# Moving the third unit's inverse, its key normalization and the first layer input's transposes in a fused delta-rule attention and MLP kernel

## The chip, the core and the metric

The kernel runs on one core of one Trainium2 chip. A core has five engines that run their own instruction lists in order: TensorE (PE in the rows, its weight loads PEld), VectorE (DVE), ScalarE (ACT), GpSimd (POOL) and SyncE (SP), which here only issues transfers. An engine waits when its next instruction needs something that another engine or a transfer has not delivered yet, and everything behind that instruction waits with it. The metric is the device time of one execution in microseconds; less is better.

## What is computed

Two stages, the second fed by the first. For each of 4 x 8 heads a 48 x 48 state is carried over 768 steps by a delta rule, and the outputs go through a two-layer MLP with a squared ReLU.

```python
B, H, S, D = 4, 8, 768, 48          # batch, heads, steps, head size
k_n = k / (norm(k, axis=-1) + 1e-06)
for t in range(S):
    y[:, :, t] = einsum('bhd,bhde->bhe', q[:, :, t], state)
    v_old = einsum('bhde,bhd->bhe', state, k_n[:, :, t])
    state += beta[:, :, t] * einsum('bhd,bhe->bhde', k_n[:, :, t], v[:, :, t] - v_old)
x = y as (3072, 384)                # 3072 tokens, d_model 384, d_ff 2048
h = maximum(x @ w_in, 0.0)
out = (h * h) @ w_out
```

## The kernel before

The 768 steps are cut into 12 units of 64 steps. For one unit the 64 sequential updates become dense products, a triangular inverse and a short chain on the carried state:

- `load` and `load_q` fetch the keys into `kpad` (three buffers in turn) and the queries into `qpad` (one buffer). `normalize` squares the keys (L290, ACT), sums (L294, DVE), takes roots and reciprocals, and scales `kpad` (L306, DVE).
- `static` turns keys and queries on TensorE (L342), copies them to `kq` (L345, ACT), forms key-key and query-key products (L358), masks them into `ap` (L368, DVE) and sends the part to be inverted through DRAM (`blocks`, L376) back into `lt` in another layout (L386). Its last step also issues the loads of the values `vt` (L247), of the next unit's queries (L253) and of the step sizes `bt` (L274, L276).
- `invert` is forward substitution on DVE: 31 steps of one multiply (L514) and one subtract (L515), then a scaling (L517). The result `z` is written to DRAM as `inv` (L521) and loaded back twice: into `tt` (L525) and `t1t` (L530). The first two units share `invert_both`, whose last part, on 16 x 16 quarters with TensorE (L468, L475), ends with the transfers `t1t` and `tt` at L488 and L493.
- `state_part` is the chain of a unit: L567 multiplies `ap` with `tt`; L604 reads the state with keys and then queries; L612 subtracts from `vt`; L578, L628, L645 and L656 follow, L650 adds to `state`, L660 copies the outputs `y`.
- `moe` is the MLP of a unit: transposes of `y` (L676), split into a high and a low part (L679, L680), first layer (L710), squared ReLU (L717, L718), split (L720, L689), second layer (L697), results (L732) to the output (L738). The matrices are split too: `split_weights` handles 28 weight pieces (`w0` to `w27`) through L141 to L173 before and during the second unit.

The order on every engine is written out by hand: the scheduler follows the order in which the program issues. Ahead of the loop this is a list of `take(part, n)`, which runs n steps of a generator. In the loop `weave` sorts the steps of all parts by a place between 0 and 1 of the unit's period, the time between two units. `steps(n, a, b)` spreads n steps evenly from a to b. The 32 steps of an inverse begin at `I0` (`J0` for the third unit, whose inverse runs in the second unit's period) and end at `I1` (`J1`), where a value above 1 means that the rest, the list `left`, falls into the unit's own period. Units are counted from one in this text, so the third unit is `u == 2` in the code.

Of the kernel before, what the change touches and what calls it, by code (L numbers as in the profile page):

```python
# [8 lines left out]
F32 = mybir.dt.float32  # L9
# [12 lines left out]
def kernel(  # L22
# [22 lines left out]
    nc = tc.nc  # L45
    B, H, S, D = q.shape
    DM, DF = w_in.shape
    P = 128
    C = 64
    HB = 32  # L50
    QB = HB // 2
    NC = 2
    NP = H // 2
# [8 lines left out]
    apool = ctx.enter_context(tc.tile_pool(name="attn", bufs=2))  # L62
# [39 lines left out]
    state = const.tile([P, 2, NC, NP, D], F32, name="state")  # L102
# [179 lines left out]
    def normalize(d):  # L282

        n2, s0, s1 = [apool.tile([P, H2], F32, name=f"{n}{d['u'] % 2}", bufs=1) for n in ("n2", "s0", "s1")]
        kn = d["kp"].rearrange("p c h d -> p (c h) d")[:, :, :D]
        squares = []
        for c in range(NC):
            sq = (apool.tile([P, H, D], F32, name="y", bufs=2) if d["u"] in (2, 3) else
                  spool.tile([P, PC], F32, name="rest", bufs=3)[:, :H * D].rearrange("p (h e) -> p h e", h=H))
            nc.scalar.activation(out=sq, in_=kn[:, c * H:(c + 1) * H], func=AF.Square)  # L290
            squares.append(sq)
# [24 lines left out]
    def static(d):  # L316

        u = d["u"]
# [3 lines left out]

        kq = apool.tile([P, NC, NP, 2, 2, C], F32, name="kq", bufs=2)
        ap = apool.tile([P, NC, H, 2, C], F32, name="ap", bufs=2)
# [102 lines left out]
    def invert_both():  # L427
# [26 lines left out]
        dd = apool.tile([P, HB, HB], F32, name="lt", bufs=1)  # L454
        nc.vector.transpose(out=dd.rearrange("p r t -> p t r"), in_=z.rearrange("p j t -> p t j"))
        parts = [dd[:, x * H2:(x + 1) * H2] for x in range(2)]
# [175 lines left out]
    def onward(d):  # L632
# [30 lines left out]
        if not u:  # L663
            for b in range(2):
                nc.scalar.copy(out=state[:, b], in_=ku[b])

# [73 lines left out]
    def take(gen, n=None):  # L740
        while n is None or n > 0:
            try:
                next(gen)
            except StopIteration:
                return
            if n is not None:
                n -= 1

    def steps(n, a, b):

        return [a + (b - a) * (m + 0.5) / n for m in range(n)]
# [32 lines left out]
    I0, I1, NI = 0.47, 1.14, HB  # L784
    J0, J1 = 0.56, 1.22
    units = S // C
    ds_ = []
# [4 lines left out]
    with tc.manual_schedule(engines=engines):  # L792
# [58 lines left out]
        take(splits, 3)  # L851
        take(chain, 1)
        take(pair[1], 1)
        load_q(ds_[2])
        take(splits, 3)
        first, third = moe(ds_[0]), normalize(ds_[2])
        take(first, 1)
        take(inverse, 1)
        take(splits, 3)
        split_early = False  # L860
        used = 6 + 2 + 3 + 4 + 3 * 3
        before = None
        corner, inverse = inverse, None
        for u in range(1, units):
            parts = []
            ends = (J0, J1) if u == 1 else (I0, I1)
            n_i = round((1 - ends[0]) / (ends[1] - ends[0]) * NI)
            if inverse:
# [3 lines left out]
            if u < units - 1:  # L872
                parts.append((static(ds_[u + 1]), [-1, 0.155, 0.165] if u > 1 else [0.16, 0.255, 0.265]))
            inverse = invert(ds_[u + 1]) if u < units - 1 else None
            if inverse:
                parts.append((inverse, steps(n_i, ends[0], 1)))
                left = steps(NI - n_i, 0, ends[1] - 1) + [ends[1] - 0.98]
            if u == 1:
                parts.append((corner, [0.03, 0.06, 0.07]))
                parts.append((third, [0.02, 0.04, 0.05, 0.075, 0.085, 0.1]))  # L880
                parts.append((late_loads(), [0.08]))
                parts.append((splits, steps(3 * (NW - FIRST) + 3 - used, 0, 0.72)))
                parts.append((pair[1], [0.25]))
# [41 lines left out]
```

## Time and profile before

| what | value |
|---|---|
| the times of three runs | 647.45, 650.03 and 936.88 us |
| their median | 650.03 us |
| the profiled execution | 647.84 us |
| its span, first to last instruction | 646.0 us |
| what lies outside the span | 1.84 us |
| mean granted TensorE clock | 0.952 |
| TensorE busy | 588.8 us (91%) |
| VectorE busy | 416.7 us (64%) |
| ScalarE busy | 317.3 us (49%) |

Times in the rows are microseconds from the span's start. [...] The span falls into a start of about 70 us, the second unit's period, in which the rest of the weights is split, up to about 150 us, and the units after that, which repeat every 45 us.

### The profile page before, as it was taken

The numbers are of one execution on the slowest core, as the hardware profiler recorded it, in microseconds if no ns is written. First come the engines' busy times: TensorE is split into PE (matmuls) and PEld (weight loads), VectorE is DVE, ScalarE is ACT, GpSimd is POOL, SyncE is SP. The second block draws the span as 40 slices with busy tenths as digits, with TensorE's granted clock in tenths as the row PEclk, the third lists the DMA queues.
The fourth block names the chain that finished last, engine by engine and source line by source line (L and its number), as shares of the span: only waits on it lengthen the run. The fifth ranks groups of instructions, "written<-read, shape, count | busy, mean of one in ns | idle before, by whom it ended". The sixth has DMA issues, their size and how long they took to land.

```text
span 646.0 us, 23872 instructions
## 1 busy us (share of the span) xinstructions
PE 588.8 (91%) x10392; PEld 557.9 (86%) x10392; DVE 416.7 (64%) x1128; ACT 317.3 (49%) x623; POOL 29.6 (5%) x52
## 2 busy tenths in 40 slices
PE   2848978994399999999999999999999999999997
PEld 2536867994399999999999999999999999999997
DVE  4785779792269488587685795794885875841121
ACT  4746766543053644545454445436445454445442
POOL 4000100000100100001001001001001010000000
PEclk9956698998599999999999999999999999999999
DMA  7787635016301722623524526217226134030100
GB/s 224 202 274 158 200 66 95 7 25 96 67 6 31 121 54 42 110 55 53 91 52 66 92 40 114 55 31 121 55 40 114 30 51 92 3 67 2 25 1 25
DMA packets 172464, 49.32 MB, mean 76 GB/s; under 512 B 164288, under 2 KB 167368, under 8 KB 172360
## 3 DMA queue, kind: packets, MB, share of 16 engines
q1 hardware_dynamic: 168840, 47.06, 36.2%
q8 instruction: 82, 1.34, 0.9%
q10 hardware_dynamic: 3392, 0.72, 0.6%
q14 instruction: 22, 0.18, 0.1%
q0 software_dynamic: 128, 0.01, 0.0%
HBM read 36.54 MB, written 10.49 MB: 73 GB/s over the span
## 4 chain that ended last, share of the span: by engine, by line
PE 81%; DVE 6%; ACT 4%; SPq 3%; DMA 3%; issue 2%; DVEq 0%; ACTq 0%
PE o L697 31%; PE h L710 30%; PE x L604 2%; PE g L604 2%; PE x L628 2%; PE x L358 2%; PE g L656 2%; PE g L358 1%; PE x L645 1%; PE x L578 1%; PE h L567 1%; PE h L676 1%; PE x L342 1%; DMA kpad<-in_k_dram 1%; PE o L166 1%
## 5 line engine op out<-in xcount | busy, mean ns | idle before, releaser
L697 PE MATMUL o<-w,h_h 128*128 128x384 f32 x768 | 204.5, 348 | 0.0
L710 PE MATMUL h<-x_h,w 128*128 128x256 f32 x1152 | 171.7, 285 | 0.0
L717 ACT ACTIVATE r<-h 128x512 f32<-128x512 f32 x96 | 57.5, 599 | 227.5 <-PE h L710 227.4
L689 DVE TENSOR_TENSOR h_l<-r,h_h 128x512 fp32r<-128x512 f32 x96 | 66.5, 692 | 147.8 <-ACT h_h L720 147.6
L710 PEld LDWEIGHTS h<-x_h,w 128*128 128x128 f32 x1152 | 156.7, 191 | 1.4 <-issue 0.2
L697 PEld LDWEIGHTS o<-w,h_h 128*128 128x128 f32 x768 | 135.1, 189 | 3.2
L697 PE MATMUL o<-w,h_l 128*128 128x384 f32 x384 | 130.6, 340 | 0.0
L710 PE MATMUL h<-x_l,w 128*128 128x256 f32 x576 | 100.9, 284 | 0.0
L514 DVE SCALAR_TENSOR_TENSOR tmp<-lt,bt,z 128x126 f32<-128x126 f32 (+22 forms) x310 | 95.8, 309 | 7.7
L515 DVE TENSOR_TENSOR z<-z,tmp 128x126 f32<-128x126 f32 (+22 forms) x310 | 79.2, 255 | 10.6
L710 PEld LDWEIGHTS h<-x_l,w 128*128 128x128 f32 x576 | 83.1, 192 | 0.0
L697 PEld LDWEIGHTS o<-w,h_l 128*128 128x128 f32 x384 | 72.7, 189 | 0.0
L718 ACT ACTIVATE r<-r 128x512 f32<-128x512 f32 x96 | 60.7, 633 | 3.0
L720 ACT CAST h_h<-r 128x512 fp32r<-128x512 f32 x96 | 59.5, 620 | 3.1
L503 POOL MEMSET z<- 128x512 f32 x10 | 5.3, 525 | 467.8 <-DMA inv<-z 434.7
L567 PEld LDWEIGHTS h<-tt,ap 32*32 32x32 f32 x704 | 7.6, 109 | 21.6 <-issue 20.5
L567 PE MATMUL h<-tt,ap 32*32 32x32 f32 x704 | 9.0, 198 | 18.7 <-DMA tt<-inv 18.7
L650 DVE TENSOR_TENSOR state<-state,x 48x384 f32<-48x384 f32 x40 | 22.0, 551 | 0.9 <-PE x L645 0.3
L358 PE MATMUL x<-kq 48*64 48x64 f32 (+1 forms) x608 | 19.1, 250 | 1.4 <-ACT kq L345 0.7
L358 PEld LDWEIGHTS x<-kq 48*64 48x64 f32 x608 | 16.6, 147 | 3.4 <-ACT kq L345 1.1
L342 PE MATMUL x<-plus,kpad 64*128 64x64 f32 x96 | 6.7, 241 | 13.9 <-DVE kpad L306 11.2
L342 PEld LDWEIGHTS x<-plus,kpad 64*128 64x128 f32 x96 | 5.4, 152 | 14.3 <-issue 11.5
(141 smaller groups left out, 651.6 us busy)
## 6 DMA issues: line engine op xcount, KB each, us to landing
w<-in_moe_w_in_dram SPq DMA_DIRECT2D x12, 512.0 KB
w<-in_moe_w_out_dram SPq DMA_DIRECT2D x16, 384.0 KB
lt<-blocks SPq DMA_DIRECT2D x20, 256.0 KB
qpad<-in_q_dram SPq DMA_DIRECT2D x96, 48.0 KB
vt<-in_v_dram SPq DMA_DIRECT2D x48, 96.0 KB
out_dram<-a SPq DMA_DIRECT2D x46, 96.0 KB
kpad<-in_k_dram SPq DMA_DIRECT2D x88, 48.0 KB
blocks<-ap SPq DMA_DIRECT2D x40, 64.0 KB
```

The lines of the kernel that those rows point to most:

```text
L358: nc.tensor.matmul(ps[j][to * C:(to + 1) * C, p, (x - first) * C:(x - first + m) * C], lhsT=kq[rows, c, p, b, 0], rhs=kq[rows, c, p, b, x: ...
L514: nc.vector.scalar_tensor_tensor(out=tmp, scalar=bt[:, s:s + 1], op0=ALU.mult, op1=ALU.mult, **factors)
L515: nc.vector.tensor_tensor(out=z[:, :nj, s + 1:], in0=z[:, :nj, s + 1:], in1=tmp, op=ALU.subtract)
L567: nc.tensor.matmul(ps[at[h % 2][b], h // 2], lhsT=ap[lower[b], c, e, 0, :HB], rhs=tt[lower[b], c, e, HB:], start=True, stop=True)
L604: nc.tensor.matmul(dst[j][to, c, p], lhsT=d["kq"][rows, c, p, b, x], rhs=state[rows, b, c, p], start=(c == 0 and p == 0) if x else True, s ...
L650: nc.vector.tensor_tensor(out=state[rows, b], in0=state[rows, b], in1=ku[b][rows], op=ALU.add)
L689: nc.vector.tensor_tensor(out=h_l, in0=r, in1=h_h.bitcast(F32), op=ALU.subtract)
L697: nc.tensor.matmul(o[i], lhsT=a[:, e, i * P:(i + 1) * P], rhs=halves["wo", ft][w], start=(ft == 0 and n == 0), stop=(ft == FT - 1 and n == 2))
L710: nc.tensor.matmul(hp[:, e], lhsT=halves["wi", (kt, ft // EACH)][w][:, f], rhs=x[:, kt], start=(n == 0), stop=(n == 3 * KT - 1))
L717: nc.scalar.activation(out=r, in_=hp, func=AF.Relu)
L718: nc.scalar.activation(out=r, in_=r, func=AF.Square)
L720: nc.scalar.copy(out=h_h, in_=r)
```

## The change

Seven things change, five of them only in the order.

- The inverse of the third unit now ends at place 1.14, as those of the other units do (`J1` is gone), and begins at 0.54 where it was 0.56. With 32 steps, 25 of them now fall into the second unit's period (21 before), 7 into the third's, and the loads of `tt` and `t1t` stand at place 0.16, ahead of the step of `static` at 0.165.
- The third unit's keys are normalized earlier: two of the six steps ahead of the loop, four at places 0.01 to 0.045. Its squares are written into `kq` of the same unit, which `static` fills later, where they were written into two `y` buffers.
- The third unit's `static` stands at 0.12, 0.2 and 0.21, where it was at 0.16, 0.255 and 0.265.
- The first layer input's transposes (`take(first, 1)`) stand right behind the copies of the first unit's `y`, ahead of the second unit's query products.
- The first unit's state is copied by DVE (line L665 before, L669 after) and no longer by ACT.
- The last part of the shared inverse stands at 0.04, 0.09 and 0.1 (0.03, 0.06, 0.07), so its loads at L488 and L493 come behind those of `late_loads` (0.08) and of the fourth unit's keys (0.09).
- The transpose at L455 is cut into two halves, the half that the matmuls at L468 read first.

```diff
         squares = []
+        if d["u"] == 2:
+            d["kq"] = apool.tile([P, NC, NP, 2, 2, C], F32, name="kq", bufs=2)
         for c in range(NC):
-            sq = (apool.tile([P, H, D], F32, name="y", bufs=2) if d["u"] in (2, 3) else
+            sq = (d["kq"][:, c].rearrange("p n i b t -> p (n i b t)")[:, :H * D].rearrange("p (h e) -> p h e", h=H)
+                  if d["u"] == 2 else apool.tile([P, H, D], F32, name="y", bufs=2) if d["u"] == 3 else
...
-        kq = apool.tile([P, NC, NP, 2, 2, C], F32, name="kq", bufs=2)
+        kq = d["kq"] if u == 2 else apool.tile([P, NC, NP, 2, 2, C], F32, name="kq", bufs=2)
...
-        nc.vector.transpose(out=dd.rearrange("p r t -> p t r"), in_=z.rearrange("p j t -> p t j"))
+        for t in (slice(QB, HB), slice(0, QB)):
+            nc.vector.transpose(out=dd[:, :, t].rearrange("p r t -> p t r"), in_=z[:, :, t].rearrange("p j t -> p t j"))
...
-                nc.scalar.copy(out=state[:, b], in_=ku[b])
+                nc.vector.tensor_copy(out=state[:, b], in_=ku[b])
...
-    J0, J1 = 0.56, 1.22
+    J0 = 0.54
...
         take(chain, 1)
+        take(splits, 1)
+        first, third = moe(ds_[0]), normalize(ds_[2])
+        take(first, 1)
+        take(splits, 2)
         take(pair[1], 1)
         load_q(ds_[2])
-        take(splits, 3)
-        first, third = moe(ds_[0]), normalize(ds_[2])
-        take(first, 1)
+        take(third, 1)
+        take(splits, 1)
+        take(third, 1)
         take(inverse, 1)
-        take(splits, 3)
+        take(splits, 2)
...
-            ends = (J0, J1) if u == 1 else (I0, I1)
-            n_i = round((1 - ends[0]) / (ends[1] - ends[0]) * NI)
+            begun = J0 if u == 1 else I0
+            n_i = round((1 - begun) / (I1 - begun) * NI)
...
-                parts.append((static(ds_[u + 1]), [-1, 0.155, 0.165] if u > 1 else [0.16, 0.255, 0.265]))
+                parts.append((static(ds_[u + 1]), [-1, 0.155, 0.165] if u > 1 else [0.12, 0.2, 0.21]))
...
-                left = steps(NI - n_i, 0, ends[1] - 1) + [ends[1] - 0.98]
+                left = steps(NI - n_i, 0, I1 - 1) + [0.16]
             if u == 1:
-                parts.append((corner, [0.03, 0.06, 0.07]))
-                parts.append((third, [0.02, 0.04, 0.05, 0.075, 0.085, 0.1]))
+                parts.append((corner, [0.04, 0.09, 0.1]))
+                parts.append((third, [0.01, 0.015, 0.03, 0.045]))
```

On SP, in the third unit's period, the transfers of its inverse (`inv`, `tt_108`, `t1t`) and those of the fourth unit (`blocks`, `lt`, `vt`) stand like this before. `out_dram<-a` is the first unit's result.

```order
L253 DMA kpad_102<-in_k_dram 64x4x48 x8
L376 DMA blocks<-ap 32x16x32 x4
L386 DMA lt<-blocks 64x1024 x2
L247 DMA vt<-in_v_dram 64x8x48 x4
L253 DMA qpad<-in_q_dram 64x4x48 x8
L274 DMA bt<-in_beta_dram 16x1x32 x4
L276 DMA bt<-bt 64x32
L521 DMA inv<-z 1024x1x32 x2
L738 DMA out_dram<-a 64x384 x4
L525 DMA tt_108<-inv 32x16x32 x4
L530 DMA t1t<-inv 32x8x32 x4
```

The same stretch of SP now, with the line numbers of the changed kernel, where they are 3 or 4 higher:

```order
L253 DMA kpad_102<-in_k_dram 64x4x48 x8
L525 DMA inv<-z 1024x1x32 x2
L379 DMA blocks<-ap 32x16x32 x4
L529 DMA tt_108<-inv 32x16x32 x4
L534 DMA t1t<-inv 32x8x32 x4
L389 DMA lt<-blocks 64x1024 x2
L247 DMA vt<-in_v_dram 64x8x48 x4
L253 DMA qpad<-in_q_dram 64x4x48 x8
```

The loads of `tt` stood behind 29 other issues from `blocks` on and now stand behind six, the two stores of `inv` among them.

On DVE, at the end of the third unit's inverse (L514, L515, L517), with the fourth unit's masking (L368), before:

```order
L515 TENSOR_TENSOR z<-z,tmp 128x15x3
L368 TENSOR_TENSOR ap<-x,mask 128x4x128 x2
L368 TENSOR_TENSOR ap<-g,mask 128x4x128 x2
L514 SCALAR_TENSOR_TENSOR tmp<-lt,bt,z 128x30
L515 TENSOR_TENSOR z<-z,tmp 128x15x2
L689 TENSOR_TENSOR h_l<-r,h_h 128x512
L514 SCALAR_TENSOR_TENSOR tmp<-lt,bt,z 128x16
L515 TENSOR_TENSOR z<-z,tmp 128x16
L732 COPY a<-o_1179 128x384
L517 TENSOR_TENSOR z<-z,bt 128x512
```

The same place of DVE now (L518, L519 and L521 are the inverse, L371 the masking):

```order
L519 TENSOR_TENSOR z<-z,tmp 128x15x3
L518 SCALAR_TENSOR_TENSOR tmp<-lt,bt,z 128x30
L519 TENSOR_TENSOR z<-z,tmp 128x15x2
L518 SCALAR_TENSOR_TENSOR tmp<-lt,bt,z 128x16
L519 TENSOR_TENSOR z<-z,tmp 128x16
L521 TENSOR_TENSOR z<-z,bt 128x512
L371 TENSOR_TENSOR ap<-x,mask 128x4x128 x2
L371 TENSOR_TENSOR ap<-g,mask 128x4x128 x2
L693 TENSOR_TENSOR h_l<-r,h_h 128x512
```

The four masking instructions, one subtraction of the MLP and the copy of a result have moved from ahead of the inverse's last instruction to behind it.

On ACT, early in the second unit's period, the copies of the third unit's turned keys and queries (L345) stand behind three eviction steps of weight pieces and two ReLU groups before (the row ahead of these is the first ReLU group's `L720`):

```order
L141 ACTIVATE w_778<-w_778 128x384
L159 CAST w_1318<-a 128x384
L168 CAST w_1166<-x 128x512
L717 ACTIVATE r<-h 128x512
L718 ACTIVATE r<-r 128x512
L720 CAST h_h<-r 128x512
L141 ACTIVATE w_780<-w_780 128x384
L159 CAST w_1370<-a 128x384
L168 CAST w_1198<-x 128x512
L345 COPY kq<-x 128x2x4x64 x2
L345 COPY kq<-g 128x2x4x64 x2
```

And now:

```order
L141 ACTIVATE w_779<-w_779 128x384
L159 CAST w_1312<-a 128x384
L168 CAST w_1175<-x 128x512
L348 COPY kq<-x 128x2x4x64 x2
L348 COPY kq<-g 128x2x4x64 x2
L721 ACTIVATE r<-h 128x512
L722 ACTIVATE r<-r 128x512
L724 CAST h_h<-r 128x512
L141 ACTIVATE w_781<-w_781 128x384
L159 CAST w_1411<-a 128x384
L168 CAST w_1203<-x 128x512
```

The copies to `kq` have moved ahead of the second ReLU group and of the eviction of weight piece 16 (`w_1198` before, `w_1203` now); on TensorE the transposes at L342 have moved in the same way, to right behind piece 15.

## Rows read from the trace of the kernel before

**Rows 1.** TensorE in order of time around its longest wait (start, us, instruction, [idle before])

```profile
152.33 0.34 PE L697 MATMUL o<-w,h_l 128*128 128x384 f32 x1
170.61 0.28 PE L567 MATMUL h<-tt,ap 32*32 32x32 f32 x2 [17.95 <-DMA tt<-inv]
171.63 1.07 PE L567 MATMUL h<-tt,ap 32*32 32x32 f32 x62 [0.74 <-DMA tt<-inv]
```

**Rows 2.** SP in order of time, 30 to 175 us (issue time, not the transfer's)

```profile
144.33 3.05 SPq L376 DMA_DIRECT2D blocks<-ap  x4
149.11 1.12 SPq L386 DMA_DIRECT2D lt<-blocks  x2
163.23 1.28 SPq L521 DMA_DIRECT2D inv<-z  x2
167.49 2.17 SPq L525 DMA_DIRECT2D tt<-inv  x4
```

**Rows 3.** The chain that ended last, 100 to 186 us (start, us, what)

```profile
169.18 2.41 DMA tt<-inv
```

**Rows 4.** Stretch 170 to 180 us: busy of each engine, granted clock, DMA share, GB/s

```profile
170.00:180.00 10.00, 8.65 (x155) 8.39 (x156) 3.26 (x11) 0.75 (x3) 0.00 (x0) 0.58 0.16 25
```

**Rows 5.** The chain that ended last, whole span: the state products of later units

```profile
220.37 1.09 PE x L604 x64
...
265.95 1.08 PE x L604 x64
```

**Rows 6.** TensorE in the fourth unit's period

```profile
219.62 0.75 PE L567 MATMUL h<-tt,ap 32*32 32x32 f32 x64
```

**Rows 7.** SP in the fourth unit's period

```profile
207.85 2.15 SPq L521 DMA_DIRECT2D inv<-z  x2
...
212.56 2.05 SPq L525 DMA_DIRECT2D tt<-inv  x4
```

**Rows 8.** DVE at the third unit's inverse, its first instruction and its end

```profile
110.32 0.24 DVE L514 SCALAR_TENSOR_TENSOR tmp<-lt,bt,z 128x31 f32<-128x31 f32 x1
...
141.83 1.28 DVE L368 TENSOR_TENSOR ap<-x,mask 128x512 f32<-128x512 f32 x2
143.02 1.28 DVE L368 TENSOR_TENSOR ap<-g,mask 128x512 f32<-128x512 f32 x2
...
145.05 0.69 DVE L689 TENSOR_TENSOR h_l<-r,h_h 128x512 fp32r<-128x512 f32 x1 [0.36 <-ACT h_h L720]
...
146.03 0.55 DVE L732 COPY a<-o 128x384 f32<-128x384 f32 x1
146.50 0.68 DVE L517 TENSOR_TENSOR z<-z,bt 128x512 f32<-128x512 f32 x1
```

**Rows 9.** TensorE in order of time, 36 to 101 us

```profile
41.30 1.90 PE L468 MATMUL h<-lt,ap 32*32 32x16 f32 x128 [1.73 <-DVE lt L455]
...
48.35 1.04 PE L475 MATMUL x<-t,h_h 16*32 16x16 f32 x60 [3.52 <-issue]
...
84.17 0.46 PE L342 MATMUL x<-plus,kpad 64*128 64x64 f32 x7 [2.67 <-ACT w L168]
...
100.80 0.75 PE L567 MATMUL h<-tt,ap 32*32 32x32 f32 x64
```

**Rows 10.** ACT in order of time, 36 to 155 us

```profile
63.57 0.86 ACT L660 COPY y<-g 128x384 f32<-128x384 f32 x2 [0.90 <-PE g L656]
...
79.80 0.59 ACT L168 CAST w<-x 128x512 fp32r<-128x512 f32 x1
...
84.86 1.08 ACT L345 COPY kq<-x 128x512 f32<-128x512 f32 x2 [0.75 <-PE x L342]
```

**Rows 11.** SP early in the second unit's period

```profile
75.72 2.60 SPq L488 DMA_DIRECT2D t1t<-lt  x4
...
89.21 5.89 SPq L253 DMA_DIRECT2D kpad<-in_k_dram  x8
```

**Rows 12.** Instructions on the third unit's key tile, issue ns min/median/max

```profile
L253 SPq DMA_DIRECT2D kpad<-in_k_dram x8: 599/620/1620, 56.0 to 62.1; - x8
```

More of the change, by code (lines that the diff above doesn't have):

```diff
@@ L852 @@
         take(chain, 1)
+        take(splits, 1)
+        first, third = moe(ds_[0]), normalize(ds_[2])
+        take(first, 1)
+        take(splits, 2)
         take(pair[1], 1)
         load_q(ds_[2])
-        take(splits, 3)
-        first, third = moe(ds_[0]), normalize(ds_[2])
-        take(first, 1)
+        take(third, 1)
+        take(splits, 1)
+        take(third, 1)
         take(inverse, 1)
-        take(splits, 3)
+        take(splits, 2)
         split_early = False
-        used = 6 + 2 + 3 + 4 + 3 * 3
+        used = 6 + 2 + 3 + 4 + 3 + 3 + 3
         before = None
@@ L872 @@
             if u < units - 1:
-                parts.append((static(ds_[u + 1]), [-1, 0.155, 0.165] if u > 1 else [0.16, 0.255, 0.265]))
+                parts.append((static(ds_[u + 1]), [-1, 0.155, 0.165] if u > 1 else [0.12, 0.2, 0.21]))
             inverse = invert(ds_[u + 1]) if u < units - 1 else None
             if inverse:
-                parts.append((inverse, steps(n_i, ends[0], 1)))
-                left = steps(NI - n_i, 0, ends[1] - 1) + [ends[1] - 0.98]
+                parts.append((inverse, steps(n_i, begun, 1)))
+                left = steps(NI - n_i, 0, I1 - 1) + [0.16]
             if u == 1:
-                parts.append((corner, [0.03, 0.06, 0.07]))
-                parts.append((third, [0.02, 0.04, 0.05, 0.075, 0.085, 0.1]))
+                parts.append((corner, [0.04, 0.09, 0.1]))
+                parts.append((third, [0.01, 0.015, 0.03, 0.045]))
                 parts.append((late_loads(), [0.08]))
```

## Prediction, on record before the changed kernel's times and trace were seen

> **What bounds the kernel now.** I read the page first: TensorE is busy 91% of the span, and in the slices behind 180 us it is never idle, so a gain has to come from the start or from the third unit. The list of TensorE's waits then has one entry that stands out, and the order of time shows it: the last matmul ends at 152.67, the next, L567 of the third unit, begins at 170.61, after 17.95 us of waiting for `tt<-inv`, and 0.74 more follow between its first two matmuls and the rest [rows 1]. [...]
>
> Why `tt` is late is read on SP. `z`, the inverse, is done on DVE at 147.18 [rows 8], but its store is issued at 163.23 only, and the load of `tt` at 167.49 [rows 2]. In between SP works off the fourth unit's transfers, beginning with `lt<-blocks` at 149.11. So the wait is a queue's, not DVE's. The last load lands 2.41 after its issue at 169.18 [rows 3], at 171.59, and TensorE goes on at once. In the fourth unit SP has another order: `inv` is issued at 207.85, as soon as `z` is there, the `tt` loads end at 212.56 + 2.05 = 214.61 [rows 7], and L567 runs at 219.62 without a wait [rows 6].
>
> Ahead of that gap TensorE works without a break from about 115 us on, so a gain made earlier passes through to 152.67 only if it is made on TensorE itself. The one long wait there is 2.67 us at L342, ended by the eviction L168 of a weight piece on ACT [rows 9].
>
> **The part that carries the forecast: the third unit's inverse.** SP now issues `inv`, four `blocks`, then `tt`. The inverse has the same 32 steps, so DVE's work up to L517 shrinks by what now stands behind it: the maskings from 141.83 to 144.30 (2.47), the subtraction L689 with the 0.36 of idle time before it (1.05), and the copy L732 up to the start of L517 (0.47) [rows 8], together 4.0 us. L517 then begins at 142.5 and ends at 143.2. From `inv`'s issue to the last `tt` issue the fourth unit needs 214.61 - 207.85 = 6.76 [rows 7]; with the landing of 2.41 [rows 3] `tt` is there at 152.4. TensorE arrives at 152.67, or 0.8 earlier by the next part, at 151.9. I take a new wait of 0.5 us. Its bounds are 0, if the steps that now begin earlier fill idle time of DVE, and 4.5, if L517 stays at 147.18: then `tt` lands at 156.35.
>
> What the old wait is worth is read from periods, because the low clock is in it: L604 begins at 220.37 in the fourth unit and at 265.95 in the fifth [rows 5], 45.58 apart. From L567 to L604 take 0.75 [rows 6]. Without the gap the third unit's L604 begins at 152.67 + 0.75 = 153.42 and the fourth's at 199.00, that is **21.4 us** earlier than 220.37. [...]
>
> [...]
>
> **The keys and `static` of the third unit.** The squares go from `y` to `kq` with the same two ACT instructions and the same two sums: 0. The buffer is free, since its last reader, the first unit's products, ran ahead of 40 us. The key load was issued by 62.7, and ACT gets to the squares at about 69. With the keys normalized earlier, the transposes L342 move ahead of one group of nine matmuls and of weight piece 16. Today they wait for that piece's eviction until 84.17 [rows 9]; piece 15 is evicted from 79.80 to 80.39 [rows 10], and L342 would follow it at about 80.8 after arriving at 80.0: 1.9 of the 2.67 are gone. But ACT now takes the four `kq` copies, two of them 1.08 [rows 10], ahead of the second ReLU group and of piece 16's eviction, and the products L358 need the bank that this eviction frees: TensorE ends L342 at 82.0, nine matmuls and the piece's products at 83.9, eighteen more at 86.1; ACT ends the copies at 84.0, the ReLU group of three at 85.9 and, after two instructions of the split, the eviction at 87.4. That is a wait of 1.3 where there are 0.6 now. Net gain 1.2.
>
> **The transposes of `y`.** They now stand right behind ACT's copies, which run from 63.57 to 64.43 [rows 10]. TensorE would reach them at 63.5 and wait 0.9; the second unit's query products, which covered that time, come later and must wait until both `h` banks are read. This costs about 0.4 on TensorE. In exchange DVE and ACT get the first layer's input 2 us earlier, which nothing on TensorE takes up, since the matmuls in front of L710 are the same. The state copy on DVE costs DVE some 1.1 where it is idle, and gives ACT 0.9 where it is not late: 0 on the path, with 0.5 either way.
>
> **The split transpose.** L468 waited 1.73 for the whole of L455 and begins at 41.30 [rows 9]; half of L455 would let it begin 1.0 earlier. Behind it L475 waits 3.52 for nothing that the profile shows, up to 48.35 [rows 9]; if that ends at a fixed time, the 1.0 is lost in it. I take 0, with bounds of -1.0 and +0.2. [...]
>
> **The shared inverse's last loads.** `t1t` and `tt` at L488 and L493 go behind the `bt`, `vt` and `kpad` issues. All of them together take SP from 75.72 to 89.21 + 5.89 = 95.10 [rows 11], and now `tt` is the last of them: it lands at 95.10 + 2.41 = 97.5 where it landed near 83. L567 of the second unit needs it at 100.80 [rows 9], or 100.0 with the gain so far. Cover of 2.5 us, cost 0.
>
> **Sum.** 647.84 (the profiled execution, 0.3% under 650.03, the median of the runs shown) - 21.4 - 1.2 + 0.4 + 0.5 = **626.1 us**.
>
> **Rivals.**
>
> The inverse is still late. DVE has no idle time from 126 to 147, so each delay there goes to L517. [...] For it: 25 steps stand in the second unit's period where 21 stood. Against: the work ahead of L517 gets less by 4.0.
>
> [...]
>
> The loads of the second unit take the place of the third's: slower than before. The 25 issues behind 75.72 took 19.4 us, 0.78 each, but one issue among the same kind of loads took 1.62 [rows 12], while weights were arriving. [...] It decides from 0.88 us an issue on, where the cover of 2.5 is used up. Against it: these issues stand behind the last weight loads and took 0.65 to 0.74 apiece.
>
> The change does not do what it says: the transfers themselves keep `tt` back, and the time stays near 647. Against it stand the fourth unit's rows [rows 6, 7].
>
> **How the numbers follow.** The forecast with its small terms (622 to 630) gets 0.66; the late inverse (632.8) 0.13; the better clock (620 to 622) 0.08; the worse start (630 to 634) 0.06; the second unit's loads 0.04, half of it with issues so slow that the time passes 661; no effect 0.03. The range 619 to 633 holds the first three and part of the fourth, 0.85 or so; its lower end is the better clock with the 1.0 of the split transpose and 0.3% of spread. A measurement tells 2%, that is 13 us, from no change: all cases down from 634.9 are faster, 0.92; the last two without that half, and the tail of the worse start, make 0.06; slower by 2%, beyond 661, 0.02.
>
> **What the changed profile would show.** Right: no wait, or less than 2 us, at the third unit's L567, at about 152; the periods of L604 from the third unit on all near 45.5; `inv` issued at about 143; clock 1.0 from 115 us to the end; L342 beginning near 81. Wrong: a wait for `tt` at the second unit's L567, near 100 us (the loads behind `kpad`); DVE ending `z` behind 146 (the late inverse); ACT waiting at the squares of the third keys; or a clock stretch of 0.5 behind 115 us.

## The result and the profile after

The changed kernel takes 627.95 us, the median of four runs (626.59 to 628.73); the kernel before, in the same series, 648.74, the median of four with one run of 936.88 among them, which the ratio leaves out. The ratio is 0.9685, with a 95% interval of 0.9648 to 0.9722: faster. The prediction said 626.1, in 619 to 633. The profiled execution took 628.73, its span 627.0 (before: 647.84 and 646.0).

The page of the changed kernel, TensorE's line and the granted clock in 40 slices:

```profile
PE 588.2 (94%) x10392; PEld 556.1 (89%) x10392; DVE 419.1 (67%) x1131; ACT 316.0 (50%) x621; POOL 29.4 (5%) x52
...
PEclk9955789799999999999999999999999999999999
```

TensorE's busy time is what it was (588.8 before); its share has risen from 91 to 94% because the span got shorter. Of the clock only the start is low (0.50 of full speed in 34.3 to 61.5, 71.8 to 82.0 and 109.4 to 116.1); behind the eighth slice, at 125 us, its mean to the end is 1.00.

TensorE in order of time where the long wait stood [rows 1]:

```profile
155.31 0.34 PE L701 MATMUL o<-w,h_l 128*128 128x384 f32 x1
155.58 0.75 PE L571 MATMUL h<-tt,ap 32*32 32x32 f32 x64
```

L571 (L567 before) has no idle time ahead of it, and all 64 run in 0.75 us. SP in the same stretch, to be laid beside [rows 2]:

```profile
145.26 1.29 SPq L525 DMA_DIRECT2D inv<-z  x2
147.62 2.56 SPq L379 DMA_DIRECT2D blocks<-ap  x4
150.37 1.96 SPq L529 DMA_DIRECT2D tt<-inv  x4
152.37 1.97 SPq L534 DMA_DIRECT2D t1t<-inv  x4
154.38 1.12 SPq L389 DMA_DIRECT2D lt<-blocks  x2
```

The store is issued 18.0 us earlier than before, the loads of `tt` 17.1. `lt<-blocks`, the first of the transfers that SP put between the finished `z` and its store, now stands behind the loads of `tt` and `t1t`; of the fourth unit's transfers only `blocks` is still ahead of them. DVE, which makes `z` [rows 8]:

```profile
112.21 0.24 DVE L518 SCALAR_TENSOR_TENSOR tmp<-lt,bt,z 128x31 f32<-128x31 f32 x1
...
144.51 0.69 DVE L521 TENSOR_TENSOR z<-z,bt 128x512 f32<-128x512 f32 x1
145.12 1.28 DVE L371 TENSOR_TENSOR ap<-x,mask 128x512 f32<-128x512 f32 x2
```

The maskings L371 stand behind the scaling L521 now; they stood ahead of it. The chain that ended last gives the beginnings of the state products in the second to fifth unit [rows 5]:

```profile
109.46 1.79 PE x L608 x43
...
156.33 1.08 PE x L608 x64
...
201.53 1.08 PE x L608 x64
...
246.98 1.08 PE x L608 x64
```

The periods are 45.20 and 45.45 from the third unit on. The fourth unit begins 18.84 earlier than at 220.37, though the second began 3.06 later than in the profiled execution of before (106.40 there). Stretch 170 to 180, where the clock was 0.58 [rows 4]:

```profile
170.00:180.00 10.00, 10.00 (x187) 9.81 (x186) 9.39 (x25) 3.79 (x7) 0.00 (x0) 1.00 0.38 76
```

Last the start, on TensorE, with the idle time ahead in brackets [rows 9]:

```profile
41.73 2.09 PE L472 MATMUL h<-lt,ap 32*32 32x16 f32 x128 [2.30 <-ACT w L141]
44.28 1.14 PE L479 MATMUL x<-t,h_h 16*32 16x16 f32 x68 [0.46 <-ACT t L474]
48.89 1.03 PE L479 MATMUL x<-t,h_h 16*32 16x16 f32 x60 [3.46 <-issue]
...
65.38 0.56 PE L660 MATMUL g<-vt,ap 64*64 64x48 f32 x24 [1.99 <-issue]
66.54 0.78 PE L680 MATMUL h<-plus,y 64*128 64x64 f32 x12 [0.59 <-ACT y L664]
...
76.31 1.73 PE L479 MATMUL x<-t1t,z 16*32 16x16 f32 x114 [2.06 <-issue]
...
82.72 0.40 PE L167 MATMUL x<-rest,plus 128*128 128x512 f32 x1
84.28 0.69 PE L345 MATMUL x<-plus,kpad 64*128 64x64 f32 x8 [1.16 <-issue]
...
103.77 0.75 PE L571 MATMUL h<-tt,ap 32*32 32x32 f32 x64
```

The wait of 2.67 for a weight piece's eviction ahead of the key transposes is gone, but one of 1.16 stands in its place, and the waits that the trace calls issue, for which it shows no releaser, have grown, this one included: 8.7 us in all, 5.1 before. In this execution the start has not become shorter.

### The profile page after: what moved, and what is told of

The parts are those of the page before. It is cut to its first block, busy times and chain, and to the rows that moved or that the text cites. A ratio compares the mean times of both kernels' runs of the same rounds, so it can differ in the third digit from the quotient of the medians.

```text
span 627.0 us, 23868 instructions
## 1 busy us (share of the span) xinstructions
PE 588.2 (94%) x10392; PEld 556.1 (89%) x10392; DVE 419.1 (67%) x1131; ACT 316.0 (50%) x621; POOL 29.4 (5%) x52
## 4 chain that ended last, share of the span: by engine, by line
PE 87%; ACT 3%; DMA 3%; DVE 2%; issue 2%; SPq 1%; ACTq 0%; DVEq 0%
PE o L701 33%; PE h L714 32%; PE x L361 2%; PE x L608 2%; PE g L608 2%; PE x L632 2%; PE g L660 2%; PE g L361 1%; PE x L649 1%; PE x L582 1%; PE x L345 1%; PE h L571 1%; PE h L680 1%; PE g L345 1%; DMA qpad<-in_q_dram 1%
## 5 line engine op out<-in xcount | busy, mean ns | idle before, releaser
L693 DVE TENSOR_TENSOR h_l<-r,h_h 128x512 fp32r<-128x512 f32 x96 | 67.9, 707 | 148.1 <-ACT h_h L724 146.7
L518 DVE SCALAR_TENSOR_TENSOR tmp<-lt,bt,z 128x126 f32<-128x126 f32 (+22 forms) x310 | 95.8, 309 | 7.8
L519 DVE TENSOR_TENSOR z<-z,tmp 128x126 f32<-128x126 f32 (+22 forms) x310 | 79.2, 255 | 10.6
L361 PE MATMUL x<-kq 48*64 48x64 f32 (+1 forms) x608 | 19.1, 251 | 1.2 <-ACT kq L348 0.7
L361 PEld LDWEIGHTS x<-kq 48*64 48x64 f32 x608 | 16.6, 147 | 3.4 <-ACT kq L348 1.1
L345 PE MATMUL x<-plus,kpad 64*128 64x64 f32 x96 | 6.7, 240 | 12.4 <-DVE kpad L309 11.3
L586 ACT ACTIVATE tt<-x 32x256 f32<-32x256 f32 x44 | 16.4, 374 | 1.4 <-PE x L582 0.8
L345 PEld LDWEIGHTS x<-plus,kpad 64*128 64x128 f32 x96 | 5.4, 152 | 13.0 <-issue 12.8
L141 ACT ACTIVATE w<-w 128x384 f32<-128x384 f32 (+1 forms) x28 | 16.6, 615 | 0.0
```

The lines of the kernel that those rows point to most:

```text
L345: nc.tensor.transpose(pair[b][:, x, p], src[rows, c, 2 * p:2 * p + 2].rearrange("p a b -> p (a b)"), ident[rows, rows])
L361: nc.tensor.matmul(ps[j][to * C:(to + 1) * C, p, (x - first) * C:(x - first + m) * C], lhsT=kq[rows, c, p, b, 0], rhs=kq[rows, c, p, b, x: ...
L518: nc.vector.scalar_tensor_tensor(out=tmp, scalar=bt[:, s:s + 1], op0=ALU.mult, op1=ALU.mult, **factors)
L519: nc.vector.tensor_tensor(out=z[:, :nj, s + 1:], in0=z[:, :nj, s + 1:], in1=tmp, op=ALU.subtract)
L693: nc.vector.tensor_tensor(out=h_l, in0=r, in1=h_h.bitcast(F32), op=ALU.subtract)
```

## The experiments

The main theory: the place of the store on SP's queue made the wait, and it alone makes the gain. Rivals: the moves in the start carry part of it; or the transfers themselves, not SP's turn, keep `tt` back.

**Only the inverse's end.** The kernel before, with this one edit:

```diff
-    J0, J1 = 0.56, 1.22
+    J0 = 0.56
...
-            ends = (J0, J1) if u == 1 else (I0, I1)
-            n_i = round((1 - ends[0]) / (ends[1] - ends[0]) * NI)
+            begun = J0 if u == 1 else I0
+            n_i = round((1 - begun) / (I1 - begun) * NI)
...
-                left = steps(NI - n_i, 0, ends[1] - 1) + [ends[1] - 0.98]
+                left = steps(NI - n_i, 0, I1 - 1) + [0.16]
```

> The kernel before with the inverse's end alone at 1.14 (beginning at 0.56), nothing else moved. If the place on SP is the whole gain and the moves at the start cost 3 us, as the changed kernel's trace reads: about 625, below the changed kernel's 627.95, with the third unit's L567 at about 152.7 and a wait there under 1 us. If the earlier keys and static are needed so that the inverse can end in time: z ends behind 146 and a wait of 3 to 5 us stands at that L567, about 631 to 633.

Measured: 628.69 us (627.25 to 630.08) against 650.15 for the kernel before in this series; 0.9665, interval 0.9632 to 0.9699. The third unit's L567 begins at 155.24 without a wait; its state products begin 45.1 ahead of the fourth's at 201.12.

```profile
155.24 0.75 PE L567 MATMUL h<-tt,ap 32*32 32x32 f32 x64
...
200.36 0.76 PE L567 MATMUL h<-tt,ap 32*32 32x32 f32 x64
```

In the start the list of waits still has the eviction:

```profile
PE x L342 <- ACT w L168: 2.7, 1, 2.7
```

One edit alone gives all of the gain: 21.5 us here and 20.8 for the whole change by the medians, and the intervals of the two ratios overlap. Neither number that was expected came: there is no wait at L567, but the moves in the start, which this kernel lacks, did not cost 3 us either.

**Everything but the inverse's end.** The changed kernel, with the old end:

```diff
-            n_i = round((1 - begun) / (I1 - begun) * NI)
+            end = 1.22 if u == 1 else I1
+            n_i = round((1 - begun) / (end - begun) * NI)
...
-                left = steps(NI - n_i, 0, I1 - 1) + [0.16]
+                left = steps(NI - n_i, 0, end - 1) + [end - 0.98]
```

> The changed kernel with the old end of the third inverse (1.22), so only the moves at the start are left. If they cost 3 us: about 651 with the wait for tt still near 18 us and the third unit's last matmul ahead of it at about 155. If they save 0.8 us, as predicted: about 647, with that matmul at about 152.

Measured: 648.66 us, 0.9973 (0.9949 to 0.9997). The wait for `tt` is back, 18.06 + 0.33. All the edits in the start together are worth 0.3%, with an interval that ends just short of nothing.

**The fourth unit's loads behind the inverse.** The kernel before, the inverse still late, but the step of `static` with the 19 transfers `lt`, `vt`, `qpad` and `bt` put behind `tt`:

```diff
-                parts.append((static(ds_[u + 1]), [-1, 0.155, 0.165] if u > 1 else [0.16, 0.255, 0.265]))
+                parts.append((static(ds_[u + 1]), [-1, 0.155, 0.245 if u == 2 else 0.165] if u > 1 else [0.16, 0.255, 0.265]))
```

> The kernel before with one step moved: the fourth unit's loads lt, vt, qpad and bt are issued behind the third unit's inverse. DVE's order is that of before, so z is still done at 147.2. If SP's queue is the cause: tt lands at about 155.5, a wait of about 3 us instead of 18, and 629 to 632. If DVE's late z or the transfers' own time is the cause, the wait stays over 10 us and the time over 640.

Measured: 633.95 us (631.46 to 634.89), 0.9741 (0.9704 to 0.9777). SP and then TensorE:

```profile
145.46 2.96 SPq L376 DMA_DIRECT2D blocks<-ap  x4
148.53 1.28 SPq L521 DMA_DIRECT2D inv<-z  x2
149.90 2.66 SPq L738 DMA_DIRECT2D out_dram<-a  x4
152.67 2.17 SPq L525 DMA_DIRECT2D tt<-inv  x4
```

```profile
155.68 0.21 PE L567 MATMUL h<-tt,ap 32*32 32x32 f32 x2 [1.89 <-DMA tt<-inv]
156.60 0.74 PE L567 MATMUL h<-tt,ap 32*32 32x32 f32 x62 [0.71 <-DMA tt<-inv]
...
203.25 0.84 PE L567 MATMUL h<-tt,ap 32*32 32x32 f32 x64
```

DVE ends `z` at 148.31, as late as ever, yet 16 us of the wait are gone: the queue kept it back, not the substitution. What is left is not DVE's alone: between the store and the loads SP now has the four stores of a result, and the loads of `tt` go out when these are issued.

The run also shows the price of a short wait. From the moment TensorE is ready for the third unit's L567 to the fourth unit's L567, 49.46 us pass here, 45.12 with the inverse alone and 66.95 in the kernel before. Less their waits of 2.60 and 18.69, the two kernels that wait are 1.7 and 3.1 us above the one that doesn't; the kernels with the inverse's old end, with the late loads and with ACT's queue below give 3.2 to 3.6 in the same way, for waits of 18.4, 13.9 and 7.8. The granted clock is 0.86 and 0.80 in the two stretches of five microseconds behind the short wait (155 to 165), and 0.50 from 170 to 178 behind the long one. The medians, 5.3 and 21.5 us above the inverse alone, agree with these sums but can't tell the two prices apart: each difference is uncertain by some 3 us.

**Early store, late loads.** The changed kernel, with only the loads of `tt` and `t1t` behind the step of `static`:

```diff
-                left = steps(NI - n_i, 0, I1 - 1) + [0.16]
+                left = steps(NI - n_i, 0, I1 - 1) + [0.17 if u == 1 else 0.16]
```

> The changed kernel with one step moved back: the store of inv stays early, the loads of tt and t1t stand behind the fourth unit's lt, vt, qpad and bt again. If the place on SP is the cause: 19 issues of 0.6 to 0.9 us and one landing come between, tt lands near 168, a wait of about 13 us plus 2.7 at the low clock, 642 to 646. If an early store is enough, under 630.

Measured: 645.53 us (643.19 to 649.42), 0.9932 (0.9892 to 0.9971). SP:

```profile
142.26 1.29 SPq L525 DMA_DIRECT2D inv<-z  x2
...
162.25 0.57 SPq L276 DMA_DIRECT2D bt<-bt  x1
162.87 2.17 SPq L529 DMA_DIRECT2D tt<-inv  x4
```

The store is out 21 us earlier than in the kernel before, and TensorE still waits 13.45 + 0.44, to 166.10. An early `z` and an early store are worth little while the loads stand behind the others.

**Another engine's queue.** The kernel before, where ACT issues the third unit's store and loads:

```diff
-            nc.sync.dma_start(out=inv...
+            (nc.scalar if d["u"] == 2 else nc.sync).dma_start(out=inv...
```

and the same at the loads of `tt` and `t1t`.

> The kernel before, with the inverse's end left at 1.22, but the third unit's store of the inverse and its loads of tt and t1t are issued by ACT instead of SP. Theory 1, the place on SP is what kept tt back: ACT has no 29 issues ahead of the store, so it goes out when z is done, near 147.2; with 6 to 7 us from the first issue to the landing of tt, tt is there at 153.5 to 156, TensorE (ready at 152.7 to 155) waits 0 to 3 us, and the time is 628 to 634. ACT holds its own work while it waits for z and for the landing of the store, 2 to 4 us; if that delays an eviction that TensorE needs, up to 638. Theory 2, the transfers themselves (the shared DMA engines) keep tt back and not SP's turn: tt still lands near 171, the wait stays above 14 us, and the time is 645 to 650.

Measured: 640.17 us (639.44 to 641.0), 0.9831 (0.9797 to 0.9865): between what the two theories gave, and 2 us above the upper end of the first. ACT in order of time (the brackets give its idle time), then TensorE:

```profile
149.84 1.32 ACTq L521 DMA_DIRECT2D inv<-z  x2
...
156.68 2.79 ACTq L525 DMA_DIRECT2D tt<-inv  x4
159.80 2.65 ACTq L530 DMA_DIRECT2D t1t<-inv  x4
162.50 0.60 ACT L717 ACTIVATE r<-h 128x512 f32<-128x512 f32 x1 [9.37 <-DMA t1t<-inv]
```

```profile
163.15 1.08 PE L567 MATMUL h<-tt,ap 32*32 32x32 f32 x64 [7.82 <-ACT r L717]
```

And the chain that ended last:

```profile
152.15 4.44 DMA lt<-blocks
156.61 0.04 ACTq L525
...
156.68 3.09 DMA tt<-inv
159.80 2.72 DMA t1t<-inv
162.52 0.59 ACT r L717
```

The store goes out at 149.84, as soon as `z` is done, where SP issued it 16 us behind `z`: so much was SP's turn. But `tt` is not there at 153.5 to 156, as the first theory had it. ACT issues the first load of `tt` at 156.68 only, when SP's `lt<-blocks` has landed: in this trace both transfers count their landing on one semaphore, and the instruction of ACT ahead of the load waits for it. By the semaphore events of the trace the last piece of `tt` lands at 162.09, so most of the 7.82 is still a wait for `tt`, and a transfer of the fourth unit still keeps it back, though not by its turn on SP. The releaser in the row, the ReLU L717, came last by 1.0 us. It frees a bank, and ACT could do it only when its issues were out, 9.37 us after its last instruction; the first theory had 2 to 4 us for this.

**The parts of the start, one by one.** Four kernels, each the changed one with one part changed, and one with two. First `y`'s transposes and the state copy at their old places:

```diff
-        take(splits, 1)
-        first, third = moe(ds_[0]), normalize(ds_[2])
-        take(first, 1)
-        take(splits, 2)
+        take(splits, 3)
         take(pair[1], 1)
         load_q(ds_[2])
+        first, third = moe(ds_[0]), normalize(ds_[2])
+        take(first, 1)
...
-                nc.vector.tensor_copy(out=state[:, b], in_=ku[b])
+                nc.scalar.copy(out=state[:, b], in_=ku[b])
```

> The changed kernel with the transposes of y at their old place, behind pieces and query products, and the state copy back on ACT. By the prediction's term these two cost 0.4 us on TensorE at L660 (measured in the trace of after: a wait of 0.59 for ACT's y): then the time is 627.2 to 628.0 where after has 627.95, no difference that can be told. If the start's end is what ACT and DVE set behind 95 us (they are saturated from 90 to 110), the later input of the first layer and the 0.9 us more on ACT cost 1 to 3 us: 629 to 631. If TensorE's waits for its own instructions set the start, nothing changes: the waits called issue still add up to 7 to 9 us, and 627 to 629.

Measured: 627.02 us (624.58 to 629.59), 0.9629 (0.958 to 0.9678).

Then the third keys and `static` at the old places:

```diff
-        take(third, 1)
...
-        take(third, 1)
...
-                ... if u > 1 else [0.12, 0.2, 0.21]))
+                ... if u > 1 else [0.16, 0.255, 0.265]))
...
-                parts.append((third, [0.01, 0.015, 0.03, 0.045]))
+                parts.append((third, [0.02, 0.04, 0.05, 0.075, 0.085, 0.1]))
```

> The changed kernel with the third unit's keys normalized, and its static step issued, at the old times. By the prediction's term the early keys are worth 1.2 us: then 629.2, with a wait of 2 to 3 us at the key transposes L345 for the eviction of a weight piece. If the waits for TensorE's own instructions, which stand at fixed places of its stream, take up what that wait loses, the wait at L345 comes back, the waits called issue fall from 8.7 to 5 or 6, and the time stays 627 to 628.5.

Measured: 628.78 us (626.72 to 629.98), 0.9652 (0.9614 to 0.969). The wait for the eviction is back, and the waits called issue fall from 8.7 to 6.2. TensorE:

```profile
83.77 0.46 PE L345 MATMUL x<-plus,kpad 64*128 64x64 f32 x7 [2.17 <-ACT w L168]
```

Then the transpose in one piece:

```diff
-        for t in (slice(QB, HB), slice(0, QB)):
-            nc.vector.transpose(out=dd[:, :, t].rearrange("p r t -> p t r"), in_=z[:, :, t].rearrange("p j t -> p t j"))
+        nc.vector.transpose(out=dd.rearrange("p r t -> p t r"), in_=z.rearrange("p j t -> p t j"))
```

> The changed kernel with the transpose of the shared inverse in one piece again. By the prediction's term of 0 for the split: 627 to 629, with L479's first issue wait shorter by as much as L472 begins later. If the split does let L472 begin 1.0 us earlier and that is kept: 629 to 630. [...]

Measured: 627.87 us (625.21 to 629.33), 0.9642 (0.961 to 0.9674). TensorE, where the numbers of lines are one lower than in the changed kernel:

```profile
42.79 1.90 PE L471 MATMUL h<-lt,ap 32*32 32x16 f32 x128 [3.46 <-DVE lt L458]
...
48.55 1.04 PE L478 MATMUL x<-t,h_h 16*32 16x16 f32 x60 [2.24 <-issue]
```

The first matmuls begin 1.06 later than at 41.73, and the issue wait behind them ends at 48.55 instead of 48.89: what the split gains is lost in that wait.

Then an attempt at a better version, with the weights' splits spread further over the second unit's period:

```diff
-                parts.append((splits, steps(3 * (NW - FIRST) + 3 - used, 0, 0.72)))
+                parts.append((splits, steps(3 * (NW - FIRST) + 3 - used, 0, 0.82)))
```

> The changed kernel with the splits of the weights in the second unit's period spread to 0.82 of it instead of 0.72. If ACT's and DVE's full load from 90 to 110 us is what ends the start (the wait of 1.92 at L608 for the eviction of a weight piece, and the low clock from 109.6 to 116.4 behind it), the wait goes and part of the low clock with it: 623 to 626. If the start's end is set by TensorE's own stream, the time stays 627 to 629. If the later splits push the third unit's inverse back on DVE, z ends later than 145.2, a wait for tt of 0.5 to 2 us comes up at the third unit's L571, and the time is 629 to 631.

Measured: 626.66 us (625.29 to 629.17), 0.9616 (0.9576 to 0.9656). The wait at L608 for the eviction did not go: 2.16 us at 107.52. At last this edit and the first of the four together, their diffs as above:

> The changed kernel with both of the edits that came out lowest by themselves: y's transposes and the state copy back at their old places, and the splits spread to 0.82 of the second unit's period. If the two gains of 1 us are real and add up, 624.5 to 626; if they are the spread of the start from run to run, 626 to 629, as the changed kernel and the others. No wait of over 1 us at the third unit's L571 is expected.

Measured: 627.52 us (625.97 to 629.0), 0.9641 (0.9616 to 0.9666). The two gains of about 1 us do not add up. The ratios of all five lie between 0.9616 and 0.9652 in series of their own, that of the changed kernel at 0.9685 and that of the inverse alone at 0.9665, with intervals of 0.25 to 0.5% to each side: none of the edits in the start can be told from no effect, and no version was found that beats the changed kernel.

**What the issue waits hang on.** Extra matmuls ahead of the first and the eighth weight piece's products in the changed kernel:

```diff
+            for _ in range(32 if x in (0, 7) else 0):
+                nc.tensor.matmul(ps[:, :32], lhsT=ident, rhs=ident[:, :32], start=True, stop=True)
```

> The changed kernel with 64 small extra matmuls (128x32, their result overwritten at once) put ahead of the first and of the eighth weight piece's products, 32 each, where TensorE waits for loads or evictions anyway (near 20 and 31 us). In the runs so far TensorE's waits called issue stood at weight loads number 493, 881, 1009, 1138 and 1266 of its stream, which are 3 x 129 and then 128 to 129 apart, whatever the order of the kernel. Theory 1, they hang on the number of instructions, since TensorE's program comes in by packets of 16,384 bytes: with the extra ones the numbers stay, and the operations move 64 pairs; the wait of 3.5 us in L479 then comes at its 5th instruction or so (number 493) instead of the 69th, that in L660 moves into L649 or L632, that in the second L479 moves ahead of it into L472. Theory 2, they hang on what the operations wait for (an event that the profile does not show): they stay at the same operations, at numbers 557, 945, 1202. The time: 626 to 630 either way, plus up to 2 us if the extra matmuls do not fit into the idle time.

Measured: 644.47 us (642.33 to 644.95), 0.9895 (0.9864 to 0.9925). It tells nothing on the question: the trace has 128 more pairs of weight load and matmul, not 64, which is one step from one wait to the next, and they took 13.86 and 10.16 us of TensorE, far more than its idle time held. The issue waits fell to 3.1 us, in a start that was 14 us longer.

With 32 small transposes ahead of the first piece only:

```diff
+            for _ in range(32 if x == 0 else 0):
+                nc.tensor.transpose(ps[:, :64], ident[:64], ident[:64, :64])
```

> The changed kernel with 32 small extra transposes (64x128 of the identity, overwritten at once) ahead of the first weight piece's products, where TensorE waits from 16.4 to 20.7 us; at the 0.06 to 0.11 us of L345's they fit into that. The 64 extra matmuls of the run before turned out as some 126 pairs in the trace, nearly the same as one step of 128 to 129, so that they could not tell the two theories apart. Theory 1, TensorE's issue waits hang on the number of instructions: the long one in the first L479 stays at weight load 493, and is now at its 37th instruction instead of its 69th; the others stay at 881, 1009, 1138, 1266, so the one of L660 moves out of L660 and the one of the second L479 into the end of L472. Theory 2, they hang on the operations: they move to 525, 913, 1041, 1170, and L479 still waits at its 69th. The time stays at 626 to 630 either way.

Measured: 628.79 us (628.45 to 631.25), 0.9697 (0.9663 to 0.9732). TensorE; L474 and L481 are L472 and L479 of the changed kernel:

```profile
47.10 0.72 PE L481 MATMUL x<-t,h_h 16*32 16x16 f32 x36 [0.48 <-ACT t L476]
50.07 1.46 PE L481 MATMUL x<-t,h_h 16*32 16x16 f32 x92 [2.26 <-issue]
...
75.70 0.30 PE L474 MATMUL x<-lt,ap 32*32 32x16 f32 x6 [4.26 <-issue]
...
86.93 0.69 PE L347 MATMUL x<-plus,kpad 64*128 64x64 f32 x8 [1.31 <-issue]
```

The wait comes ahead of the 37th of the 128 matmuls (it was the 69th), at number 493 as before, counted over TensorE's weight loads and semaphore instructions together. The one of the second L479 (now L481) has moved into the end of L474, at number 1137, the one in L660 is gone from there, and a wait of 0.79 has come up at number 621, which is 128 behind 493. That is the first theory, with 32 pairs more ahead: these waits keep to the same counts and change their instruction. The one at the key transposes (L345, here L347) does not: it stood at number 1278 and is now at 1309, so it has moved with its instruction.

## Why the prediction was right

**What bounds the kernel** was read rightly: nearly all of the wait was a queue's, not DVE's. The kernel with the fourth unit's loads behind the inverse has a late `z` and loses only 2.60; the one with an early store and late loads keeps 13.89 of the wait.

**The third unit's inverse, -21.4 and +0.5.** In the profiled executions the fourth unit's state products begin 113.97 behind the second's before and 92.07 after: 21.9 less. The inverse alone gave 21.5 in time. The working from periods, with the low clock in it, was right; less the two waits of 18.69 it leaves 2.7 for the matmuls at the low clock (0.50 from 170 to 178 in the kernel before), and by the traces of the kernel before and of the inverse alone these are 3.1. DVE's way from the first step to the end of the scaling shrank from 36.86 to 32.99, by 3.9 (forecast 4.0). From the store's issue to the last of `tt` SP took 7.07 (forecast 6.76). `z` ends at 145.20 and not at 143.2 because the inverse began 1.9 later. The 0.5 for a new wait was too careful: TensorE came to L571 at 155.58, 3.7 later than forecast, and the last load, issued at 151.83, had landed at 154.16 by the semaphore events of the trace. Some 1.4 us of cover is left; it is thin, since a wait of 2.60 cost 4.3 with the clock of 0.86 and 0.80 behind it.

**The keys and `static`, -1.2.** In the trace this term came out otherwise than it was put. The transposes L345 no longer wait for the eviction, as forecast, but they begin at 84.28 and not near 81: TensorE comes to them at 83.12, where the forecast had 80.0, and then waits 1.16. Every kernel with the early keys has such a wait there, of 0.8 to 1.6; in the kernels with the late loads and with the splits spread further the trace names the weight piece's product L167 just ahead as its releaser. The forecast had put nothing in its place. The loss that it did put against the gain, a wait of 1.3 for the next eviction at L361 (L358 before), was 0.45. The other issue waits add up to 7.5 in the changed kernel, but to 4.5 to 7.5 in all the kernels with the early keys and to 5.1 to 6.5 in those with the old ones (without the two that have extra matmuls); that they take up what the eviction's wait gave back is not shown. Nor is -1.2 refuted as a figure, since the timed difference is within its spread: the edits of the start together measured -1.8 us alone (0.0027 of 650.15, interval -0.2 to -3.3), and +1.3 by the medians of the changed kernel and the inverse alone, each against its own series.

**The transposes of `y`, +0.4.** The wait for ACT's copies is there, 0.59 at L680 (forecast 0.9). Its removal gives no difference that can be measured. The state's two copies took 0.55 us each on DVE (L669) and 0.50 each on ACT before (L665).

**The split transpose, 0.** Right, and the pair of traces agrees with the reason given: the 1.06 is gained and lost in a wait behind it. One pair shows no more than that, since the starts of single executions differ by as much. The two halves took 2.17 on DVE against 2.05 for the whole, 0.12 more. The upper bound of +0.2 was the author's estimate and no run shows it; what the traces show in its place is this 0.12.

**The shared inverse's loads, 0.** SP issues them here:

```profile
91.81 3.36 SPq L492 DMA_DIRECT2D t1t<-lt  x4
95.27 2.60 SPq L497 DMA_DIRECT2D tt<-lt  x4
```

They end at 97.87, 2.8 later than forecast, and L571 of the second unit runs at 103.77 without a wait. An issue took 0.65 to 0.84, below the 0.88 from which this rival would have decided; what slower issues would have cost, up to a time beyond 661, was the author's estimate and was not shown. The forecast's 0.65 to 0.74 for the kernel before left out the four issues of `vt`, which took 0.80 there.

**The rivals.** The late inverse was priced at 632.8, the 626.1 with 4.0 more of wait and 2.7 for a low clock behind it. No run shows the 2.7 behind a wait of 4.5; behind the one of 2.60 the runs showed 1.7, at clocks of 0.86 and 0.80. The kernel that has the late inverse, without the queue, took 633.95. That is partly luck: its wait was 2.60 where 4.5 was priced, and the sum that the price was added to lies 2.6 below the inverse alone. The better clock, put at 620 to 622, did not come: ahead of the gap the kernel before had 0.50 in 35.2 to 58.9, 65.8 to 72.6, 76.0 to 79.3 and 106.9 to 113.5, and the changed kernel had it in 34.3 to 61.5, in 71.8 to 82.0 and again in 109.4 to 116.1. The profiled execution of the kernel with `y`'s transposes at the old place had 1.00 in the last of these stretches. Its L571 of the third unit begins at 151.77 and not at 155.58, 1.2 of it gained before that stretch, and it took 625.04; the other 2.6 us go with that one stretch. The times given to the better clock and to the worse start (630 to 634) were the author's estimates; beyond these 2.6 no run shows them. That transfers themselves keep `tt` back is refuted by the inverse alone: with the store and the loads of the round trip put ahead of the fourth unit's `lt`, `vt`, `qpad` and `bt` the time went from 650.15 to 628.69. Moving the issues to ACT gained 10 us where moving them ahead on SP gained 21: there `tt` still waited for one of SP's transfers to land.

**The sum** came out 2.6 below the profiled execution and 1.9 below the median. Of this the start is the larger part, which the prediction took 0.8 shorter. In the profiled executions the second unit's state products began anywhere between 106.40 and 109.46, in both orders (106.40, 108.70, 108.78 and 108.99 with the old start; 107.12, 107.54 and 109.46 with the new), so the 3 us by which the start looks worse in the one trace of after are spread, and no effect of the order is shown. The sum also started from the earliest of these executions, 647.84, where fourteen later runs of the kernel before have a median of 650.15; that it came so near is in part luck. The gain is the better test: forecast 21.7, measured 20.4 by the ratio (18.0 to 22.8). It bears out the 21.4; the small terms are too small for it to tell.

## What to carry to other kernels

When an engine waits for a load, look when the load and the store ahead of it were issued and what their queue did from the moment the data was there; if it issued other things, the gain is to be had by order alone, and both halves of a round trip have to be moved: here the time was 645.53 with the store alone early and 627.95 with both. Another engine's queue need not free them: on ACT the first load went out at 156.68 only, when SP's `lt<-blocks` had landed at 156.59. Price a wait by the distance of a later milestone to one without the wait, so that the low clock behind it is counted; here a wait of 2.6 us cost 1.7 more than its length, and waits of 7.8 to 18.7 cost 3.1 to 3.6 more. A saved wait in a stretch with other waits is not yet a gain: look whether the next one ends at a time of its own, and whether another comes up in its place.

## What the runs showed of the hardware

TensorE's issue waits in the start, all but one, stand at set counts of its instructions and end shortly after a packet of one queue has landed. The page names that queue instruction (packets, MB, share of 16 engines):

```profile
q8 instruction: 82, 1.34, 0.9%
```

That is 16.3 KB a packet, 82 of them. The changed kernel's trace has 10392 weight loads, each with its matmul, and 173 semaphore and drain instructions of TensorE, which is 128.8 a packet; the kernel with 128 pairs of weight load and matmul more has 83 packets. Counted over the weight loads and semaphore instructions of a trace, the waits stand at numbers 493, 881, 1009, 1138 and 1266 (and 621 in the last run above), 128 to 129 or three times as much apart, in kernels with the instructions in different orders. They end 1.2 to 1.9 us after such a packet has landed, and 32 instructions put ahead left the numbers where they were and moved the waits to other matmuls. The trace names no releaser for them, so that TensorE waits for the packet is inferred from this agreement. The exception is the wait at the key transposes: it ends 4.7 to 5.9 us after the last packet and moved with its instruction. The waits show in the start, where hundreds of matmuls of 16 to 64 columns follow each other; behind it there are few, of up to 1.0 us, and the second layer's matmuls, of 384 columns, have none. What decides how long a single wait is (0.3 to 4.3 us here) was not tried, and stays open.
